# Hash-masked attention and a mixture of experts in one launch: the order of POOL's work before the first expert, and where the raw pieces of its w2 are kept

## The chip, the cores and the metric

The kernel runs on one core of one Trainium2 chip, as one program. The metric is the device time of an execution in microseconds (us); the median of three runs of the kernel before is 697.48 us (697.29 to 697.7).

Engines are named as in the profile: PE is the matmul engine (PEld its weight loads), DVE is VectorE, ACT is ScalarE, POOL is GpSimd, SP issues most of the DMAs. Each engine works through its own queue in order.

## The reference

Attention over 4 batches x 8 heads, 768 tokens, head size 64. A query sees a key only where the signs of six projections of the two agree. Its output is a matrix x of 3072 tokens x 512, and each token goes to the expert with the highest gate logit:

```python
scores = scale * np.matmul(q, k.transpose(0, 1, 3, 2))
scores = np.where(mask, scores, -1000000000.0)          # mask: equal buckets
attn = np.exp(scores - np.max(scores, axis=-1, keepdims=True))
attn = attn / (np.sum(attn, axis=-1, keepdims=True) + 1e-09)
x = np.matmul(attn, v)                                   # then 3072 x 512
...
e_idx = np.argmax(x @ w_gate, axis=1)
for e in range(E):
    h = np.maximum(x[mask] @ w1[e], 0.0)                 # 512 x 1024
    ye = h @ w2[e]                                       # 1024 x 512
    out[mask] = gate_w[mask, None] * eom[mask, e, None] * ye
```

## The kernel before

All matrix products are in float32 accuracy by way of two parts: an operand is split into a rounded high part (a copy to the type fp32r) and a low part (operand minus high part), and three products are summed.

**Attention.** The 32 heads are worked on as 16 pairs, and each pair in 12 steps, 192 steps in all. A step is one 128 x 768 block of scores: PE makes the scores (line 612), VectorE takes them out of PSUM with a row minimum (line 615), ScalarE takes the exponential and the row sums (line 623), POOL multiplies by the reciprocal of the row sums (`normal`, line 633), PE transposes the block six steps later (line 662), ScalarE, and VectorE for some, copy the transposes into the tiles `pts0` and `pts1` (lines 664 and 669), and after each six steps PE multiplies them by v (`weighted`, line 680). `normal` handles two steps at a time. In every block of six steps POOL normalises four tiles at the block's first step and two more at its fifth. Here a *tile* is such a 128 x 768 block.

**The order.** Nothing is left to a scheduler: the program is issued in the order in which it is written. `plan(step, fn)` puts a piece of work behind a step, `block(step, when, fn)` puts it at a place of the first step of a block of six (`early`, `amid`, `before`, `matmuls`, `behind`). `late` is 168. The last two blocks begin at steps 186 and 192; step 192 holds no new scores, only what is still in flight.

**The seam.** The expert with the most tokens of the first three batches is chosen at step 172 and is worked on first, with the first 256 of its tokens. During the last blocks of attention the kernel gathers these tokens (`early_gather`, step 186, two indirect DMAs issued by POOL once VectorE has made their numbers `gid`), loads the four pieces of the expert's w1 (`early_load`, 512 KB each, issued by SP into two buffers `w_raw` in turn, so piece 2 waits for the splits of piece 0 and piece 3 for those of piece 1), and splits each piece in two halves of 512 columns into high and low parts on POOL (`early_w1(cc, h)`, lines 1014 and 1015). Below, half (1,1) is the second half of piece 1.

After step 192's block the first products of the expert begin: `fill(f)` is a 128 x 256 block of x @ w1 and `low` takes its low part out of PSUM (line 369). Between them stand the last `weighted` products, the last logits (`add_pair`, lines 735 and 736), and the routing of the last batch on VectorE (`best`, line 743 is the subtraction `df`; `choose` to `ohb`; `prefix` on PE, line 797). The four pieces of w2 (two row blocks of 128 each, 512 KB) are loaded by `w2_piece` just behind `fill(0)`: two raw pieces into a spare buffer of `pts0`, two into `w_raw`. Their high and low parts are shared out by `split_weights` (lines 180 to 183): "h" puts the high part on POOL, otherwise ScalarE has it; "l" puts the low part on POOL, otherwise VectorE has it.

For every later expert, raw pieces of w1 and w2 go in turn into four buffers (two `w_raw`, `xh0`, `xlo0`); the turn is counted by the list `raws`, which grows only where `load_weights` gets no buffer handed in.

Of the kernel before, what the change touches and what calls it, by code (L numbers as in the profile page):

```python
# [21 lines left out]
P = 128  # L22
NT = S // P
HS = S // 2
DM = H * D
# [34 lines left out]
def lsh_attention_then_moe(  # L60
# [375 lines left out]
    with ExitStack() as actx:  # L436
# [24 lines left out]
        def plan(step, *fns):  # L461
            at.setdefault(step, []).extend(fns)
# [164 lines left out]
        def normal(s0):  # L627

            rs = sp.tile([P, GROUP], F32, name="rsum")
            nc.vector.tensor_reduce(rs, sums.pop(s0 // GROUP), AX.X, ALU.add)  # L630
            nc.vector.reciprocal(rs, rs)
            for k in range(GROUP):
                nc.gpsimd.tensor_scalar(live[s0 + k], live[s0 + k], rs[:, k:k + 1], 0.0, ALU.mult, ALU.add)  # L633

        def transposed(s, pr):
            g, hf, t, j = tile_of(s)
# [370 lines left out]
        def early_load(cc):  # L1007
            early.setdefault("raw", []).append(w1_load(0, cc))
            early.setdefault("w1", []).append([wpool.tile([P, F], F32R, name="w1" + n, bufs=NCC) for n in "hl"])

        def early_w1(cc, h):
            c = slice(h * F // 2, (h + 1) * F // 2)
            hi, lo, raw = (x[:, c] for x in (*early["w1"][cc], early["raw"][cc]))
            nc.gpsimd.tensor_scalar(hi, raw, 1.0, 0.0, ALU.mult, ALU.add)
            nc.gpsimd.tensor_tensor(lo, raw, f32(hi), ALU.subtract)

        plan(late + 2, compare, pick)
# [2 lines left out]
        for a in range(EARLY):  # L1020
            block(late + 24, ("early", "amid")[a], lambda a=a: early_turn(a))
        for cc in range(NCC):
            plan(late + (4, 5, 11, 15)[cc], lambda cc=cc: early_load(cc))
            for h in range(2):
                if cc >= NCC // 2 and h:
                    block(late + 24, "behind", lambda cc=cc, h=h: early_w1(cc, h))
                else:
                    plan(late + (9, 10, 13, 14, 18, 0, 20)[2 * cc + h], lambda cc=cc, h=h: early_w1(cc, h))

        with tc.manual_schedule(engines=MANUAL | {mybir.EngineType.SP}):  # L1030
            t = signs()
# [92 lines left out]
                lows.pop(0)()  # L1124

            fill(0)
            spare = tp.tile([P, NT, HS], F32, name="pts0").rearrange("p a b -> p (a b)")
            pieces = {}
            for f in (4, 6, 0, 2):
                raw = spare[:, (f - 4) * DM:(f - 2) * DM].rearrange("p (f d) -> p f d", f=2) if f >= 4 else None  # L1130
                pieces[f] = w2_piece(ep, 0, f, "h" if f >= 4 else "l", raw)
            for f in range(0, NFB, 2):
                w2s += pieces[f]
            for c in range(NT):
                weighted(2 * NP - 1, c)
                if c == 0:
# [249 lines left out]
```

## Time and profile before

| what | value |
|---|---|
| median of 3 runs | 697.48 us (697.29 to 697.7) |
| the profiled execution | 696.61 us |
| its span, first to last instruction | 694.9 us |
| DVE, ACT, POOL busy | 460.9, 440.0, 417.9 us (66, 63, 60%) |
| granted PE clock, mean | 0.998 of full speed |
| DMA, mean over the span | 126 GB/s |

Busy times are of the profiled execution. Attention takes up to about 376 us of it, the experts the rest. Times in the rows further down are us from the start of the span; a row gives the start, the length of the group in us, the engine, the line, the operation, what it writes and reads, a count, and in brackets the engine's idle time ahead of it with what ended that.

### The profile page before, as it was taken

To read this page: it belongs to the slowest core of one execution; us is meant where nothing else is said; L and a number is where in the kernel's file an instruction comes from. 1 tells how busy PE (TensorE), PEld (TensorE's weight loads), DVE (VectorE), ACT (ScalarE), POOL (GpSimd) and SP (SyncE) were. 2 spreads that over 40 slices of the span, in tenths; PEclk is the share of its full clock that TensorE was granted. 3 is DMA by queue.
4 is the path that set the end of the run, shared out by engine and by line. 5 is a ranking of instruction groups with operands and counts; after the bars stand their busy time and mean duration, and the time that the engine had idled before them with its cause. 6 is when DMAs were issued, how large, how long until landed. Compare 5 with 4: busy or idle time off the path is not lost. (4 is left out here: it accounts for less than half of the span.)

```text
span 694.9 us, 17362 instructions
## 1 busy us (share of the span) xinstructions
PE 683.1 (98%) x6591; PEld 539.3 (78%) x6591; DVE 460.9 (66%) x1012; ACT 440.0 (63%) x896; POOL 417.9 (60%) x548
## 2 busy tenths in 40 slices
PE   8999999999999999999999999999999999999996
PEld 5667676767666766666666888889999999989896
DVE  7888887888887889788876934462536354556440
ACT  5988998889888988888986224433435252434231
POOL 6767766587856678657899447163372827374201
PEclk9999999999999999999999999999999999999999
DMA  5554554364444444443444136533455444535401
GB/s 175 150 129 98 129 130 97 75 141 112 110 118 99 117 99 121 99 99 73 134 112 139 34 122 207 208 109 117 142 167 167 164 159 165 171 126 212 153 11 44
DMA packets 85283, 87.47 MB, mean 126 GB/s; under 512 B 57167, under 2 KB 67591, under 8 KB 85192
## 3 DMA queue, kind: packets, MB, share of 16 engines
q1 hardware_dynamic: 79704, 72.88, 38.5%
q0 software_dynamic: 5200, 13.31, 5.8%
q8 instruction: 54, 0.88, 0.5%
q14 instruction: 37, 0.30, 0.1%
q10 hardware_dynamic: 288, 0.10, 0.1%
HBM read 59.57 MB, written 13.11 MB: 105 GB/s over the span
## 5 line engine op out<-in xcount | busy, mean ns | idle before, releaser
L633 POOL TENSOR_SCALAR sc<-sc,rsum 128x768 f32<-128x768 f32 x192 | 171.9, 911 | 79.9 <-ACT pts L669 40.2
L615 DVE TENSOR_SCALAR_CACHE_REDUCE sc<-ps_s 128x768 f32<-128x768 f32 x192 | 176.3, 955 | 24.1 <-PE ps_s L612 22.3
L623 ACT ACTIVATE sc<-sc,mn 128x768 f32<-128x768 f32 x192 | 178.9, 951 | 3.8 <-DVE sc L615 3.7
L612 PE MATMUL ps_s<-kh,qhl 64*128 64x384 f32 x768 | 148.2, 400 | 1.4 <-DVE sc L615 0.8
L680 PE MATMUL ps_a<-pts,vt 128*64 128x384 f32 x768 | 131.2, 490 | 0.0
L669 ACT COPY pts<-ps_t 128x384 f32<-128x384 f32 x188 | 93.0, 494 | 25.3 <-PE ps_s L662 22.0
L369 DVE SCALAR_TENSOR_TENSOR hl<-ps_s,hh 128x256 fp32r<-128x256 f32 (+8 forms) x40 | 34.0, 849 | 107.6 <-ACT hh L368 107.6
L680 PEld LDWEIGHTS ps_a<-pts,vt 128*64 128x64 f32 x768 | 52.5, 137 | 66.3 <-issue 60.9
L380 POOL DMA_INDIRECT out_dram<-yo,sid x29 | 30.7, 1059 | 113.9 <-ACT yo L375 52.2
L662 PEld LDWEIGHTS ps_t<-ident,sc 64*128 64x128 f32 x1140 | 81.9, 139 | 22.1 <-POOL sc L633 13.2
L358 PE MATMUL ps_s<-xh,w1h 128*128 128x256 f32 (+7 forms) x288 | 96.8, 336 | 0.4 <-DVE hl L369 0.4
L332 POOL DMA_INDIRECT xq<-x_dram,idx x75 | 82.2, 1096 | 23.8 <-issue 21.0
L358 PE MATMUL ps_s<-xlo,w1h 128*128 128x256 f32 (+7 forms) x288 | 95.4, 331 | 0.0
L358 PE MATMUL ps_s<-xh,w1l 128*128 128x256 f32 (+7 forms) x288 | 95.3, 331 | 0.0
L662 PE MATMUL ps_t<-ident,sc 64*128 64x64 f32 x1140 | 86.9, 223 | 1.3 <-POOL sc L633 1.3
L368 ACT ACTIVATE hh<-ps_s 128x256 fp32r<-128x256 f32 (+8 forms) x40 | 29.0, 726 | 90.4 <-PE ps_s L358 90.4
L612 PEld LDWEIGHTS ps_s<-kh,qhl 64*128 64x128 f32 x768 | 76.2, 187 | 4.4 <-DVE sc L615 2.2
L612 PE MATMUL ps_s<-kl,qhl 64*128 64x384 f32 x384 | 66.6, 333 | 0.0
L612 PE MATMUL ps_s<-bb 64*128 64x384 bf16 x384 | 65.3, 327 | 0.0
L669 ACT COPY pts<-ps_m 128x384 f32<-128x384 f32 x94 | 45.1, 480 | 17.5 <-PE ps_m L662 16.1
L358 PEld LDWEIGHTS ps_s<-xh,w1h 128*128 128x128 f32 x288 | 54.2, 188 | 2.3 <-issue 0.6
L358 PEld LDWEIGHTS ps_s<-xlo,w1h 128*128 128x128 f32 x288 | 54.2, 188 | 1.4 <-DVE xlo L315 0.2
(250 smaller groups left out, 1388.4 us busy)
## 6 DMA issues: line engine op xcount, KB each, us to landing
w_raw<-in_w_dram SPq DMA_DIRECT2D x34, 512.0 KB
qk<-in_qkT_dram SPq DMA_DIRECT2D x32, 384.0 KB
qhl<-qhl SPq DMA_DIRECT2D x62, 192.0 KB
xh<-in_w_dram SPq DMA_DIRECT2D x14, 512.0 KB
xlo<-in_w_dram SPq DMA_DIRECT2D x14, 512.0 KB
vt<-in_v_dram SPq DMA_DIRECT2D x16, 384.0 KB
x_dram<-xb SPq DMA_DIRECT2D x60, 96.0 KB
xq<-x_dram,idx POOLq DMA_INDIRECT x75, 3.0
```

The lines of the kernel that those rows point to most:

```text
L332: nc.gpsimd.indirect_dma_start(out=xq[:, k * P:(k + 1) * P], out_offset=None, in_=x_dram.rearrange("n (a f) -> (n a) f", a=NB32), in_offse ...
L358: nc.tensor.matmul(ps, l, r, start=first and k == 0, stop=last and k == len(pairs) - 1)
L368: nc.scalar.activation(hh, ph, AF.Relu)
L369: return lambda: nc.vector.scalar_tensor_tensor(hl, ph, 0.0, f32(hh), ALU.max, ALU.subtract)
L380: nc.gpsimd.indirect_dma_start(out=out[:, :], out_offset=bass.IndirectOffsetOnAxis(ap=sid[0:n, r, a:a + 1], axis=0), in_=yo[0:n], in_offse ...
L612: nc.tensor.matmul(ss[:, h, 0:HS], q[rs, c:c + P], k[rs, 0:HS], start=(i == 0), stop=(i == 3))
L615: nc.vector.tensor_scalar(sc, ss[:, :, 0:HS], MASKED, None, ALU.min, ALU.min, accum_out=mn)
L623: nc.scalar.activation(pr, pr, AF.Exp, bias=mn, scale=-1.0, accum_out=sums[s // GROUP][:, k, 0:1])
L633: nc.gpsimd.tensor_scalar(live[s0 + k], live[s0 + k], rs[:, k:k + 1], 0.0, ALU.mult, ALU.add)
L662: nc.tensor.transpose(trs[h][:, c], pr[r, c * P:(c + 1) * P], ident[r, r])
L669: (nc.vector.tensor_copy if h and s and (last or s % PER == 0) else nc.scalar.copy)(pts[:, :, t * P + h * hq:t * P + (h + 1) * hq], trs[h])
L680: nc.tensor.matmul(st["av"][j * D:(j + 1) * D], st["v"][:, j, c], blocks[hb][j][:, c], start=(c == 0), stop=(c == NT - 1))
```

## The change

Four edits in the seam:

1. Half (1,1) of w1 moves from step 182 to step 186, behind the gathers and three tiles. The load of piece 3 moves from step 183 to step 186, behind that half.
2. One tile, step 184, is normalised by VectorE.
3. The high part of half (2,0) moves to ScalarE, and the half from step 186 to 187. Halves (2,1) and (3,1) move from the block of step 192 to behind the w2 pieces.
4. All four raw pieces of w2 go into spare buffers `pts0` and `pts1`. POOL makes the high parts of the first two, ScalarE those of the other two, and VectorE all four low parts. With two fewer entries in `raws`, every later piece takes the buffer two further on in the ring.

```diff
             for k in range(GROUP):
-                nc.gpsimd.tensor_scalar(live[s0 + k], live[s0 + k], rs[:, k:k + 1], 0.0, ALU.mult, ALU.add)
+                e = nc.vector if s0 + k == NSTEP - PER - GROUP else nc.gpsimd
+                e.tensor_scalar(live[s0 + k], live[s0 + k], rs[:, k:k + 1], 0.0, ALU.mult, ALU.add)
...
             hi, lo, raw = (x[:, c] for x in (*early["w1"][cc], early["raw"][cc]))
-            nc.gpsimd.tensor_scalar(hi, raw, 1.0, 0.0, ALU.mult, ALU.add)
+            if (cc, h) == (2, 0):
+                nc.scalar.copy(hi, raw)
+            else:
+                nc.gpsimd.tensor_scalar(hi, raw, 1.0, 0.0, ALU.mult, ALU.add)
             nc.gpsimd.tensor_tensor(lo, raw, f32(hi), ALU.subtract)
...
         for cc in range(NCC):
-            plan(late + (4, 5, 11, 15)[cc], lambda cc=cc: early_load(cc))
+            plan(late + (4, 5, 11, 18)[cc], lambda cc=cc: early_load(cc))
             for h in range(2):
-                if cc >= NCC // 2 and h:
-                    block(late + 24, "behind", lambda cc=cc, h=h: early_w1(cc, h))
-                else:
-                    plan(late + (9, 10, 13, 14, 18, 0, 20)[2 * cc + h], lambda cc=cc, h=h: early_w1(cc, h))
+                if cc < NCC // 2 or h == 0:
+                    plan(late + (9, 10, 13, 18, 19, 0, 20)[2 * cc + h], lambda cc=cc, h=h: early_w1(cc, h))
...
             fill(0)
-            spare = tp.tile([P, NT, HS], F32, name="pts0").rearrange("p a b -> p (a b)")
-            pieces = {}
-            for f in (4, 6, 0, 2):
-                raw = spare[:, (f - 4) * DM:(f - 2) * DM].rearrange("p (f d) -> p f d", f=2) if f >= 4 else None
-                pieces[f] = w2_piece(ep, 0, f, "h" if f >= 4 else "l", raw)
+            spare = [tp.tile([P, NT, HS], F32, name=f"pts{n}").rearrange("p a b -> p (a b)") for n in range(2)]
             for f in range(0, NFB, 2):
-                w2s += pieces[f]
+                raw = spare[f // 4][:, f % 4 * DM:(f % 4 + 2) * DM].rearrange("p (f d) -> p f d", f=2)
+                w2s += w2_piece(ep, 0, f, "h" if f < 4 else "", raw)
+            for cc in (2, 3):
+                early_w1(cc, 1)
```

The order on POOL, from half (1,0) of w1 on (`sc` are tiles, `w1h` and `w1l` the parts of a half, `xg` the gathers, `w2h` and `w2l` the parts of w2 pieces). Before:

```order
L1014 TENSOR_SCALAR w1h<-w_raw 128x512
L1015 TENSOR_TENSOR w1l<-w_raw,w1h 128x512
L1014 TENSOR_SCALAR w1h<-w_raw 128x512
L1015 TENSOR_TENSOR w1l<-w_raw,w1h 128x512
L633 TENSOR_SCALAR sc<-sc,rsum 128x768 x2
L295 DMA xg<-x_dram,gid_7521 128x512 x2
L633 TENSOR_SCALAR sc<-sc,rsum 128x768 x4
L1014 TENSOR_SCALAR w1h<-w_raw 128x512
L1015 TENSOR_TENSOR w1l<-w_raw,w1h 128x512
L1014 TENSOR_SCALAR w1h<-w_raw 128x512
L1015 TENSOR_TENSOR w1l<-w_raw,w1h 128x512
L633 TENSOR_SCALAR sc<-sc,rsum 128x768 x6
```

The same place after the change, on to the w2 pieces and the two halves behind them:

```order
L1018 TENSOR_SCALAR w1h<-w_raw 128x512
L1019 TENSOR_TENSOR w1l<-w_raw,w1h 128x512
L634 TENSOR_SCALAR sc<-sc,rsum 128x768 x2
L295 DMA xg<-x_dram,gid_7515 128x512 x2
L634 TENSOR_SCALAR sc<-sc,rsum 128x768 x3
L1018 TENSOR_SCALAR w1h<-w_raw 128x512
L1019 TENSOR_TENSOR w1l<-w_raw,w1h 128x512 x2
L1018 TENSOR_SCALAR w1h<-w_raw 128x512
L1019 TENSOR_TENSOR w1l<-w_raw,w1h 128x512
L634 TENSOR_SCALAR sc<-sc,rsum 128x768 x6
L180 TENSOR_SCALAR w2h<-pts_7893 128x1024 x2
L1018 TENSOR_SCALAR w1h<-w_raw 128x512
```

The pair of tiles and the gathers have moved up by one half, and a tile has gone from the four. Half (1,1), the low part of (2,0) and half (3,0) stand together ahead of the last six tiles. The last row begins half (2,1), which now stands behind the w2 high parts; the two low parts of w2 that followed them on POOL are gone.

On VectorE, at the last transposes of attention and the start of the routing of the last batch (`pts` copies end the attention, `w2l` are low parts of w2 pieces, `lgt` the logits, `hl` low parts of `fill`). After the change:

```order
L670 COPY pts_7776<-ps_t 128x6x64
L728 TENSOR_REDUCE lgt<-ps_t 128x48
L183 TENSOR_TENSOR w2l<-pts_7893,w2h 128x1024 x2
L183 TENSOR_TENSOR w2l<-pts_7894,w2h 128x1024 x2
L693 STREAM_TRANSPOSE xb<-ot 128x384
L737 TENSOR_TENSOR lgt<-lgt,ps_m 128x48
L684 COPY ot<-ps_a 128x384
L369 SCALAR_TENSOR_TENSOR hl<-ps_s,hh 128x256
L737 TENSOR_TENSOR lgt<-lgt,ps_m 128x48
```

Before, one row of two low parts stood there; now there are two such rows. All of them stand ahead of the copy of `ot`, which PE needs for the last logits.

On SP, from the load of piece 2 of w1 to the raw pieces of w2 (`x_dram<-xb` writes x). After the change:

```order
L173 DMA w_raw<-in_w_dram 128x1024
L700 DMA x_dram<-xb 32x24x32 x4
L173 ISA
L173 DMA w_raw<-in_w_dram 128x1024
L700 DMA x_dram<-xb 32x24x32 x4
L163 ISA
L163 DMA pts_7893<-in_w_dram 128x1024
```

The rows are those of before in the same order; the second `w_raw` row (piece 3) now waits for half (1,1) at its new place, and the four loads of w2 behind it all go to `pts`.

## Rows read from the trace of the kernel before

**Rows 1.** The page, busy time of each engine.

```profile
PE 683.1 (98%) x6591; PEld 539.3 (78%) x6591; DVE 460.9 (66%) x1012; ACT 440.0 (63%) x896; POOL 417.9 (60%) x548
```

**Rows 2.** Busy time by stretch, 391 to 690 us; columns as the first line says.

```profile
core 0: us, PE busy (x) PEld busy (x) DVE busy (x) ACT busy (x) POOL busy (x), PEclk, DMA share, GB/s
391.00:690.00 299.00, 298.68 (x1638) 278.18 (x1637) 143.70 (x190) 108.53 (x135) 132.68 (x135) 1.00 0.43 142
```

**Rows 3.** Timeline of PE, its waits in the seam.

```profile
364.15 0.27 PE L662 MATMUL ps_t<-ident,sc 64*128 64x64 f32 x1 [0.84 <-POOL sc L633]
365.03 0.27 PE L662 MATMUL ps_t<-ident,sc 64*128 64x64 f32 x1 [0.29 <-POOL sc L633]
...
389.95 0.20 PE L797 MATMUL ps_m<-ohb,tri 128*128 128x48 bf16 x1 [0.84 <-DVE ohb L762]
...
390.74 0.39 PE L358 MATMUL ps_s<-xh,w1h 128*128 128x256 f32 x1 [0.44 <-DVE hl L369]
```

**Rows 4.** Timeline of POOL, from half (1,1) on.

```profile
356.68 0.62 POOL L1014 TENSOR_SCALAR w1h<-w_raw 128x512 fp32r<-128x512 f32 x1
...
358.68 1.79 POOL L633 TENSOR_SCALAR sc<-sc,rsum 128x768 f32<-128x768 f32 x2
360.66 1.21 POOL L295 DMA_INDIRECT xg<-x_dram,gid  x1 [0.19 <-issue]
...
363.18 3.55 POOL L633 TENSOR_SCALAR sc<-sc,rsum 128x768 f32<-128x768 f32 x4
```

**Rows 5.** Timeline of DVE, the gathers' numbers, and from the w2 low parts on.

```profile
357.80 0.92 DVE L957 CAST gid<-o_gd 128x2 uint32<-128x2 f32 x1
...
380.88 3.18 DVE L183 TENSOR_TENSOR w2l<-pts,w2h 128x1024 fp32r<-128x1024 f32 x2 [2.96 <-POOL w2h L180]
...
384.57 0.54 DVE L683 COPY ot<-ps_a 128x384 f32<-128x384 f32 x1
...
386.90 1.82 DVE L743 TENSOR_TENSOR df<-lgt,mx 128x48 f32<-128x48 f32 x1
```

**Rows 6.** Timeline of POOL, half (3,0), the last six tiles, the w2 parts.

```profile
368.66 0.62 POOL L1014 TENSOR_SCALAR w1h<-w_raw 128x512 fp32r<-128x512 f32 x1
...
370.63 5.31 POOL L633 TENSOR_SCALAR sc<-sc,rsum 128x768 f32<-128x768 f32 x6
...
379.80 2.05 POOL L180 TENSOR_SCALAR w2h<-pts 128x1024 fp32r<-128x1024 f32 x2
383.19 5.46 POOL L183 TENSOR_TENSOR w2l<-w_raw,w2h 128x1024 fp32r<-128x1024 f32 x2 [1.34 <-ACT w2h L182]
```

**Rows 7.** Timeline of ACT, high parts of two w2 pieces.

```profile
382.06 1.05 ACT L182 CAST w2h<-w_raw 128x1024 fp32r<-128x1024 f32 x1 [2.63 <-DMA w_raw<-in_w_dram]
384.52 1.05 ACT L182 CAST w2h<-w_raw 128x1024 fp32r<-128x1024 f32 x1 [1.41 <-DMA w_raw<-in_w_dram]
```

**Rows 8.** Timeline of SP, loads of w1 piece 3 and of two w2 pieces.

```profile
358.72 0.36 SPq L173 DMA_DIRECT2D w_raw<-in_w_dram  x1
...
377.92 0.33 SPq L173 DMA_DIRECT2D w_raw<-in_w_dram  x1
...
379.86 0.33 SPq L173 DMA_DIRECT2D w_raw<-in_w_dram  x1
```

**Rows 9.** Busy time by stretch, from the issue of piece 3's load on.

```profile
358.72:361.75 3.03, 3.03 (x40) 1.54 (x38) 1.22 (x6) 1.67 (x6) 2.84 (x3) 1.00 0.50 173
```

**Rows 10.** Timeline of PE, the last tile's transposes and the last logits.

```profile
376.35 0.59 PE L662 MATMUL ps_s<-ident,sc 64*128 64x64 f32 x12
...
385.43 0.75 PE L735 MATMUL ps_m<-wgt,ot 128*128 128x32 f32 x6
```

**Rows 11.** Timeline of DVE at the start of the kernel.

```profile
8.37 1.25 DVE L546 SCALAR_TENSOR_TENSOR qhl<-qk,qhl 128x384 fp32r<-128x384 f32 x1
```

**Rows 12.** Timeline of POOL at the same time.

```profile
8.02 1.19 POOL L548 TENSOR_TENSOR kl<-qk,kh 128x384 fp32r<-128x384 f32 x1
9.18 0.81 POOL L555 TENSOR_SCALAR qhl<-qk 128x384 fp32r<-128x384 f32 x1
9.96 0.51 POOL L556 TENSOR_SCALAR kh<-qk 128x384 fp32r<-128x384 f32 x1
```

## The prediction

> **What bounds the kernel now.** I read the page's totals first, then the releasers of the matmul engine's idle time, then the timelines of the engines around those waits. PE is busy for 683.1 us of a 694.9 us span [rows 1]: only removing PE idle time can help. From 391 us to the end PE shows 298.68 us busy in 299 [rows 2], so what the change does to the later experts can gain nothing, and what it moves must pay in the seam between attention and the first expert. There PE has four large idle entries [rows 3]: 0.84 and 0.29 us at 364 to 365, waiting for softmax tiles that POOL normalises, and 0.84 and 0.44 us at 390, waiting for VectorE's routing chain: 2.41 us together. The others in the seam are 0.2 us or less. That is the whole stake, plus what each wait hides at an engine's start.
>
> The POOL timeline [rows 4] says why PE waits at 364: the second half of w1 piece 1 (its high part from 356.68, then its low part) stands ahead of a pair of tiles at 358.68, then come two gathers from 360.66, and only at 363.18 the tiles that PE wants. The VectorE timeline [rows 5] says why PE waits at 390: the subtraction `df` takes 1.82 us on 48 columns, from 386.90 to 388.72, and it ends as POOL's two w2 low parts end, 383.19 + 5.46 = 388.65 [rows 6].
>
> **The change, step by step.**
> *POOL before the load.* Half (1,1) leaves, so the tile pair starts at 356.68 and ends 1.79 later, at 358.47 [rows 4]. The gathers need `gid`, which VectorE ended at 357.80 + 0.92 = 358.72 [rows 5]; that cast sat beside POOL's instruction too, and I keep 358.72. With 0.2 us to start, the gathers run from 358.9; they took 363.18 - 360.66 = 2.52 us, so 361.4. Three tiles instead of four, 3.55 / 4 = 0.89 each: 364.1. PE wants the first of them at 364.15 - 0.84 = 363.3, and it is there at 362.3, so the waits of 0.84 and 0.29 go. The fourth tile lies on VectorE, which at that time waits for PE: nothing on PE's path. ScalarE's new cast (half of the 1.05 us of a whole piece [rows 7], about 0.55) stands ahead of four PSUM copies of the tiles that are now early; ScalarE had to wait for those tiles before, so this too costs PE nothing against before.
>
> *The wait that the change adds.* Piece 3 of w1 is now loaded after half (1,1), whose raw buffer it takes over. High and low part of a half take 370.63 - 368.66 = 1.97 us [rows 6]: (1,1) ends at 364.1 + 1.97 = 366.1, and SP can issue the load only then; before, it was issued at 358.72 [rows 8], some ten us ahead of POOL's reader at 368.66. Now the reader, the high part of (3,0), comes right behind it, and **behind that stand the last six softmax tiles**. How long does the load take? No row shows a lone load with its waiting reader, so by bounds: the one issued at 358.72 had traffic until 361.75 (173 GB/s for 3.03 us, which is 524 KB) [rows 9], so 3.0 us at least; for the ones issued at 377.92 and 379.86 ScalarE waited until 382.06 and 384.52 [rows 7, 8], 4.14 and 4.66 us. I take 4.14, the reader that waited least: 370.2. The low part of (2,0) fits into that wait. Then (3,0), 1.97: 372.2, and six tiles, 5.31 [rows 6]: **377.5, where before they ended at 370.63 + 5.31 = 375.9**. PE's transposes of the last tile start at 377.5, not 376.35 [rows 10]; with their 0.59 us what follows starts at 378.1. Before, it was 0.17 us later than that after them, behind ScalarE's copy, at 377.1. PE has lost its gain and is 1.0 us behind. It is due at the last logits (line 735) at 385.43 + 1.0 = 386.4.
>
> *The low parts of w2.* POOL goes on with two high parts, 2.05 us [rows 6]: 379.5. VectorE now has four low parts. Two took 3.18 us from 380.88, but the first stood until POOL's casts ended (379.80 + 2.05 = 381.85), so they take (384.06 - 381.85) / 2 = 1.1 us each [rows 5, 6]. Against them POOL now runs halves (2,1) and (3,1). Do they overlap? At the start of the kernel VectorE's operation at 8.37 takes 1.25 us beside POOL's at 8.02, and POOL's next, dispatched at 9.18, takes 0.81 where the same shape takes 0.51 at 9.96 [rows 11, 12]: the two engines took turns, and the waiting one came in although the other had its next one queued. I take turns here too: 4 x 1.1 + 0.62 + 1.35 + 0.62 = 7.0 us (a half's 1.97 less its high part's 0.62 are the 1.35), so 386.5. Ahead of PE's logits come then a transpose and the copy of `ot`; from the end of the low parts at 384.06 to the end of that copy, 384.57 + 0.54, it was 1.05 us [rows 5]: 387.55, and PE starts at 387.6, not 386.4: a **new wait of 1.2 us**, 2.2 us behind before.
>
> *What is paid back.* From 385.43 to 390.74 PE needed 5.31 us, of which 0.84 + 0.44 idle [rows 3, 10]: 4.03 of work. The chain on VectorE is shorter: POOL's long low parts are gone, and of the 1.82 us of `df` all but 0.07 lie before their end, so I take 1.6 off, and the 389.95 - 385.43 = 4.52 us to the end of the chain become 2.9. Ready at 390.5, wanted some 3 us after 387.6, at 390.6 or later: hardly a wait. PE stands at 387.6 + 4.03 = 391.6 where it was at 390.74: +0.9.
>
> *The buffers.* The raw pieces of later experts change places in a ring of four; the first two of expert 1 go to `w_raw` and are loaded earlier. PE is not idle there [rows 2], so nothing.
>
> **Sum:** -1.1 (waits at 364) + 2.1 (late last tiles) + 1.2 (low parts) - 1.3 (waits at 390) = +0.9 us. The profiled execution took 696.61 us, so 697.5; the median of the runs is 0.87 above it, so **698.4**. About 0.2% (1.4 us) is what a measurement of this kernel tells from no change, so this reads as the same.
>
> The Trainium skill ("SBUF — State Buffer", section "SBUF: two separate sides") says that a VectorE instruction with two SBUF inputs and a POOL instruction that reads SBUF contend for a port pair, an exclusive lock that whichever starts first holds for its whole instruction. The trace agrees: 1.82 us for `df`. By that rule the sum stands as it is; if the engines overlapped, it would be rival A's.
>
> **Rivals.**
> *A, VectorE keeps the upper hand for its four low parts.* For it: its second low part followed the first although POOL had asked at 383.19 [rows 5, 6]. Against it: rows 11 and 12. They end at 379.5 + 4.4 = 383.9, the copy of `ot` is in time, the logits run at 386.4, and PE stands at 386.4 + 4.03 = 390.4: -0.3, **697.2**.
> *B, faster: A and a quick load.* With the load at its lower bound, 3.0 us, all POOL times come 1.1 earlier: -0.3 - 1.1 = -1.4, and 0.2 more if the gathers start at once: **695.9**. It decides below a load of some 3.1 us. Against it: both reads of rows 7.
> *C, slower: the gathers and the load both meet company.* VectorE's new tile falls on the first gather; its price lies between nothing and the 0.89 us that POOL took for such a tile. The x writes that follow on SP's queue can stretch the load to 4.66. A tenth on POOL is a tenth at the end: +0.9 with 0.5 for each is +1.9, with all of both +2.3: **699.4 to 699.8**. It decides once half a us is added. For it: the first gather took 1.21 us [rows 4].
> The Trainium skill (same page and section, the trap "DVE blocks DMA") says that POOL is kept from writing a gather's descriptors while VectorE runs a two-port operation; no run here shows it for this tile.
> *D, the gathers do not move.* If something other than POOL's queue held them at 360.66, all of POOL is 1.8 later: +2.7, **700.2**, and the change would not do what it says.
>
> **Chances.** Forecast 0.40, A 0.18, B 0.10, C 0.27, D 0.05. Faster by over 0.2%: B and a little of A, 0.12. Slower by over 0.2%: C, D and the upper end of the forecast (a load of 4.66 us), 0.40. Within: 0.48. The range leaves out the quicker part of B, D and the end of C: 696.1 to 700.0. The forecast's own, with the load between 3.7 and 4.66 us, is 698.0 to 698.9.
>
> **What would show it.** Right: no PE wait at 364; POOL idle for about 3 us in front of the high part of (3,0), released by the load; PE idle between the transposes of the last six tiles; PE waiting for the copy of `ot` ahead of the last logits; `df` at 0.2 us and no wait for the end of its chain. Wrong: if POOL waits under 2 us for the load, or the four low parts run in 4.5 us, the time is under 697.5; if the first of the three tiles starts after 362, it is over 699.

## The result, and the profile after

The change makes the kernel **slower**: 702.58 us (median of 6, 700.49 to 704.0) against 697.98 us for the kernel before on the same chip, a ratio of 1.0062 (95% interval 1.0048 to 1.0077). The forecast was 698.4 us, its range ended at 700.0. The profiled execution is the quickest of the six, 700.49 us with a span of 698.8 us: 3.9 us more than before's.

PE's idle time, as in [rows 1, 2]: first the page's totals, then the stretch from 391 us on (columns as in [rows 2]).

```profile
PE 684.2 (98%) x6591; PEld 539.6 (77%) x6591; DVE 462.9 (66%) x1015; ACT 439.9 (63%) x897; POOL 414.7 (59%) x544
```

```profile
391.00:690.00 299.00, 296.94 (x1623) 276.34 (x1623) 142.88 (x190) 108.09 (x135) 132.79 (x135) 1.00 0.43 142
```

Before, PE idled 0.32 us in that stretch; now 2.06 us, in a part of the kernel in which no line of code was changed. The timeline of PE shows its waits (the answer to [rows 3]; three more like the first ones are left out):

```profile
373.14 0.59 PE L663 MATMUL ps_t<-ident,sc 64*128 64x64 f32 x12 [0.39 <-POOL sc L634]
374.03 0.59 PE L663 MATMUL ps_s<-ident,sc 64*128 64x64 f32 x12 [0.30 <-POOL sc L634]
...
377.55 0.59 PE L663 MATMUL ps_s<-ident,sc 64*128 64x64 f32 x12 [0.29 <-POOL sc L634]
...
387.00 0.86 PE L736 MATMUL ps_m<-wgt,ot 128*128 128x32 f32 x6 [0.45 <-DVE ot L684]
...
409.71 0.72 PE L306 MATMUL ps_t<-ident,xg 128*128 128x128 f32 x4 [2.06 <-DMA xg<-x_dram,gid]
```

The waits at 364 and 390 are gone, the last six tiles come late one after another, the copy of `ot` is late: the seam, as forecast. The last line is new and was not forecast: PE waits for a gather, the second half of the first expert's later tokens (`xg`).

POOL in the seam, which answers to [rows 4, 6]:

```profile
356.74 1.78 POOL L634 TENSOR_SCALAR sc<-sc,rsum 128x768 f32<-128x768 f32 x2
358.85 1.30 POOL L295 DMA_INDIRECT xg<-x_dram,gid  x1 [0.33 <-DVE rsum L631]
...
361.46 2.68 POOL L634 TENSOR_SCALAR sc<-sc,rsum 128x768 f32<-128x768 f32 x3
...
370.21 0.62 POOL L1018 TENSOR_SCALAR w1h<-w_raw 128x512 fp32r<-128x512 f32 x1 [2.88 <-DMA w_raw<-in_w_dram]
...
372.17 5.32 POOL L634 TENSOR_SCALAR sc<-sc,rsum 128x768 f32<-128x768 f32 x6
...
379.48 1.59 POOL L1018 TENSOR_SCALAR w1h<-w_raw 128x512 fp32r<-128x512 f32 x1
381.15 2.11 POOL L1019 TENSOR_TENSOR w1l<-w_raw,w1h 128x512 fp32r<-128x512 f32 x1
```

and VectorE ([rows 5]):

```profile
378.80 7.10 DVE L183 TENSOR_TENSOR w2l<-pts,w2h 128x1024 fp32r<-128x1024 f32 x4
...
386.40 0.54 DVE L684 COPY ot<-ps_a 128x384 f32<-128x384 f32 x1
...
388.57 0.21 DVE L744 TENSOR_TENSOR df<-lgt,mx 128x48 f32<-128x48 f32 x1
```

SP's loads ([rows 8]): piece 3 of w1, then what matters, the first two loads of the second expert:

```profile
366.12 0.36 SPq L173 DMA_DIRECT2D w_raw<-in_w_dram  x1
...
401.66 1.01 SPq L173 DMA_DIRECT2D w_raw<-in_w_dram  x2
```

Before, SP issued no load between 392 and 422.95 us (there `xh` was the first). The DMA issues between 399 and 412 us, first of before, then of the change (tile, queue, count, KB each for loads, median us to landing):

```profile
xg<-x_dram,gid POOLq DMA_INDIRECT x5, 3.4
out_dram<-yo,sid POOLq DMA_INDIRECT x2, 2.9
```

```profile
w_raw<-in_w_dram SPq DMA_DIRECT2D x2, 512.0 KB
xg<-x_dram,gid POOLq DMA_INDIRECT x4, 6.8
out_dram<-yo,sid POOLq DMA_INDIRECT x1, 6.2
```

Gathers and the scatter take twice as long beside 1 MB of loads. The Trainium skill ("DMA: Bandwidth & Descriptors", section "Issuing engines are not separate DMA queues") says that DMAs of different issuing engines run on the same 16 DMA engines and interleave; these rows agree.

### The profile page after: what moved, and what is told of

It is laid out like the page before. It is cut to its first block, busy times and chain, and to the rows that moved or that the text cites. A ratio compares the mean times of both kernels' runs of the same rounds, so it can differ in the third digit from the quotient of the medians.

```text
span 698.8 us, 17358 instructions
## 1 busy us (share of the span) xinstructions
PE 684.2 (98%) x6591; PEld 539.6 (77%) x6591; DVE 462.9 (66%) x1015; ACT 439.9 (63%) x897; POOL 414.7 (59%) x544
```

## The experiments

Theory T: the loads at 401.66 are the loss. Rival S: the seam's own new waits are. C and D are about the spread of the executions, O and P about how the loads do harm, T2 about the program's end. All times are medians, beside before on the same chip; chips differ by up to 2.7 us for before. The ratio is estimated from the executions and need not be the quotient of the two medians.

| run | us | before | ratio (95%) |
|---|---|---|---|
| e1_ring_back | 699.62 | 698.79 | 1.0019 (1.0006 to 1.0033) |
| e2_ring_only | 698.98 | 698.79 | 1.0006 (0.9992 to 1.0021) |
| e3_loads_held | 699.58 | 698.79 | 1.0025 (1.0009 to 1.0041) |
| e4_tiles_first | 699.75 | 698.79 | 1.0025 (1.0013 to 1.0037) |
| a2_change_again | 703.15 | 698.78 | 1.0068 (1.0042 to 1.0094) |
| e6_ring_and_gap | 699.05 | 698.78 | 0.9998 (0.9983 to 1.0013) |
| e7_gather_early | 701.44 | 698.78 | 1.0039 (1.0024 to 1.0053) |
| e5_two_lows_late | 698.44 | 698.78 | 0.9996 (0.9981 to 1.0010) |
| b2_before_again | 697.36 | 698.24 | 0.9993 (0.9981 to 1.0005) |
| e8_lows_placed | 697.21 | 698.24 | 0.9993 (0.9978 to 1.0007) |
| e9_pe_kept_busy | 701.12 | 698.24 | 1.0048 (1.0028 to 1.0069) |
| e10_placed_ring | 702.28 | 698.24 | 1.0065 (1.0039 to 1.0090) |
| e13_before_no_rounds | 700.27 | 700.65 | 0.9991 (0.9978 to 1.0005) |
| e12_change_no_rounds | 701.59 | 700.65 | 1.0021 (1.0006 to 1.0035) |
| e14_seam_alone | 700.75 | 700.65 | 1.0004 (0.9989 to 1.0019) |
| e11_pick_early | 699.02 | 700.65 | 0.9974 (0.9962 to 0.9986) |
| a3_change_third | 703.22 | 698.50 | 1.0059 (1.0041 to 1.0076) |
| e1b_ring_back_again | 699.01 | 698.50 | 1.0016 (1.0003 to 1.0028) |

To see where in the span each profile gains or loses, I lined the traces up: the start of the 181st score tile on VectorE (344.0 us in before) is taken as zero, and the table gives how far PE's results are behind before's (us; less is earlier) at the end of ScalarE's relu of the eighth fill, of the first product behind the fills, at the dispatch of the last scatter, and the time from there to the span's end (before: 4.33).

| profile | eighth fill | next product | last scatter | rest |
|---|---|---|---|---|
| the change | -0.05 | +2.26 | +2.26 | 5.89 |
| a2_change_again | +1.43 | +2.99 | +4.25 | 5.85 |
| a3_change_third | +0.95 | +5.00 | +5.02 | 6.04 |
| e1_ring_back | +0.82 | +0.83 | +0.87 | 5.72 |
| e1b_ring_back_again | +2.20 | +2.23 | +2.26 | 5.94 |
| e3_loads_held | +0.97 | +0.97 | +0.97 | 5.90 |
| e2_ring_only | +0.01 | +0.05 | +0.96 | 5.69 |
| e6_ring_and_gap | +0.03 | +0.54 | +1.94 | 4.32 |
| e7_gather_early | +0.43 | +0.46 | +2.08 | 5.98 |
| e4_tiles_first | +0.98 | +1.00 | +1.02 | 5.79 |
| e8_lows_placed | -2.32 | -2.33 | -1.14 | 5.70 |
| e10_placed_ring | -2.35 | -2.38 | +4.05 | 6.11 |
| e11_pick_early | -2.38 | -2.35 | -0.51 | 5.86 |

### Is it the loads or the seam?

**e1_ring_back**, and again beside the change itself as **e1b_ring_back_again**; the edit is one line behind the loop over w2's pieces:

```diff
                 w2s += w2_piece(ep, 0, f, "h" if f < 4 else "", raw)
+            raws += [0, 1]
```

> The change as it is, but the ring of raw buffers goes on where it did before: expert 1's first two loads go to xh0 and xlo0 again and so are issued at some 423 us, not 401.66. Theory T (the two loads at 401.66 run beside the gathers of the first expert's last tokens, which land after up to 7.4 us instead of 3.5, and PE waits 2.1 us for them at 409.7): that wait is gone, no load is issued on SP between 392 and 420 us, and the time is that of before, 697.0 to 698.5 us. Rival S (the ring costs nothing, as predicted; the seam's own new waits are the loss): as the change, 701 to 703 us.

> The change with the ring set back, beside the change on the same chip. Theory T (the early loads are the largest part of the loss, by the gathers and scatters that they slow): 2 to 4 us under the change, 0.5 to 2.0 us over before, of which 1.4 us are the program's end by the profiles and the rest the seam's. If the ring is worth what the two runs without the unused block say (0.8 us): 3 us or more over before, within 1.5 us of the change.

The change's own third run stood beside the second of these:

> The change once more, on the same chip as the run with the ring set back, to have the ring's price from one chip. Whatever the chip, 4 to 5 us over before if the program's end (1.5 us in the profiles), the early loads and the seam add up as in the first two comparisons (1.0062 and 1.0068).

With the list two entries longer, the second expert's loads start in `xh0` again, are issued at 424.29, and the gathers land after 3.6 us (e1: SP's first load behind 396 us, then the DMA issues between 399 and 412 us):

```profile
424.29 0.39 SPq L173 DMA_DIRECT2D xh<-in_w_dram  x1
```

```profile
xg<-x_dram,gid POOLq DMA_INDIRECT x4, 3.6
out_dram<-yo,sid POOLq DMA_INDIRECT x2, 3.0
```

On one chip: change 703.22, ring set back 699.01, before 698.50. **By the medians the ring is worth 4.2 us of the 4.7 us that the change loses there**; rival S falls. The size is less sure than the cause: the executions spread over 2.9 us (the change, 6 of them) and 4.1 us (e1b, 12), and their means differ by 2.9 us. e1 lay 1.1 us over theory T's upper end, e1b 0.2 us outside one of its ranges and at the lower edge of the other: a loss of 0.5 to 0.8 us stays without the loads.

**e3_loads_held** keeps the ring and holds the loads until the tokens have landed:

```diff
+        for i in range(2):
+            held = wpool.tile([P, F], F32, name="w_raw", bufs=2)
+            nc.sync.dma_start(held[0:1, 0:4], xg[1][0][0:1, 0:4])
```

> The change, with its ring, but the two loads are held until the first expert's gathered tokens have landed: 16 bytes of them are copied into each w_raw buffer first, so that the loads have to wait for that. Theory T: the gathers land after 3.5 us as before, the loads are issued at about 406 to 408 us, PE does not wait at 409, and the time is 697.0 to 699.0 us. Rival S: as the change, 701 to 703 us. If the gathers' lateness comes from something other than the loads, it stays in this run and goes in none of those that keep the change's seam.

The loads go out at 408.84, the gathers land after 3.7 us, PE does not wait for them: 699.58, like e1 and not like the change, though half a us over the range. So it is the moment of the loads, not the buffer they go to.

**e2_ring_only** is before with the ring turned (`del raws[-2:]` behind the same loop).

> The kernel before with one thing of the change alone: the ring of raw buffers is turned by two, so that expert 1's first two loads go to w_raw. Theory T: the loads are issued at about 400 us, PE waits about 2 us for the gathered tokens at about 409, and the time is 2 to 5 us over before: 699.5 to 702.5 us. Rival S: as before, 697.5 to 698.5 us.

A miss of theory T as it stood: 698.98, 0.2 us over before and not told apart from it. The loads were issued at 401.94 and the gathers landed after 5.9 us, yet PE did not wait for them. Its profile loses 0.9 us later on, since POOL's scatter waited for the slowed one ahead of it and `pick`, POOL's copy of a selection matrix that stands behind it, came late (timeline of PE):

```profile
416.07 1.08 PE L324 MATMUL ps_t<-tacc,pick 128*128 128x32 f32 x8 [0.62 <-POOL pick L320]
```

### Why the same loads hurt the change and not before

The two gathers and VectorE's rows around them, in before and in the change (timelines of DVE and POOL):

```profile
399.39 0.17 DVE L957 CAST gid<-o_gd 128x2 uint32<-128x2 f32 x1
...
399.80 0.41 DVE L982 TENSOR_REDUCE tacc<-o_tt 128x32 f32<-128x256 f32 x1
...
399.83 1.02 POOL L295 DMA_INDIRECT xg<-x_dram,gid  x1 [3.68 <-DVE gid L957]
401.16 0.95 POOL L295 DMA_INDIRECT xg<-x_dram,gid  x1 [0.30 <-issue]
```

```profile
399.26 0.42 DVE L983 TENSOR_REDUCE tacc<-o_tt 128x32 f32<-128x256 f32 x1
399.59 0.16 DVE L958 CAST gid<-o_gd 128x2 uint32<-128x2 f32 x1
...
399.99 0.60 DVE L981 TENSOR_TENSOR o_tt<-tacc_e,perm 128x256 f32<-128x256 f32 x1
...
400.03 1.41 POOL L295 DMA_INDIRECT xg<-x_dram,gid  x1 [3.81 <-DVE gid L958]
401.75 0.95 POOL L295 DMA_INDIRECT xg<-x_dram,gid  x1 [0.30 <-issue]
```

In the change the reduction stands ahead of the cast `gid`. No line of that code differs: behind the seam VectorE's order is not simply the written one, as my description of the kernel had it (in before, too, a first `o_tt` runs at 398.68, ahead of the cast that is written before it). The next two-input operation, `o_tt`, is then already running when the first gather starts, and the gather takes 1.41 us instead of 1.02, in every profile with that order. So the second gather is dispatched 0.09 us behind the loads, where in e2 it is 0.73 ahead of them (401.21 and 401.94). Of these 0.82 us the longer gather makes 0.39; it also starts 0.15 later, and the loads go out 0.28 earlier. The Trainium skill ("SBUF — State Buffer", section "SBUF: two separate sides", the trap "DVE blocks DMA") says that POOL cannot write a gather's descriptors while VectorE runs an operation in a two-port mode, such as a copy. `o_tt` is a product of two SBUF inputs, which the trap does not name; the row shows a delay of that kind for it too, 0.39 us.

**e7_gather_early** puts the cast back ahead in the change:

```diff
+            nc.vector.tensor_copy(tacc[0:1, 0, 0, 0:1], gid0[0:1, 0:1])
             for i in (0, 2, 1):
```

> The change with its ring and its seam, but VectorE casts the gather's numbers ahead of the reduction of the expert table, as before (one element of the table is first written from those numbers). In the change the cast stands behind that reduction, and a VectorE operation with two inputs runs over the first gather, which takes 1.41 instead of 1.02 us. Theory O: the first gather is dispatched at 399.8 and takes 1.0 us, the second is dispatched at about 401.2, ahead of the loads at 401.7, it lands after about 6 us, PE waits less than 0.5 us at 409, and the time is 1.5 to 2.5 us under the change's: 699 to 700.5 us. Rival P (the loads alone, whatever the order): PE still waits about 2 us, and the time is the change's.

The first gather takes 1.02 us, the second is dispatched 0.94 us ahead of the loads, PE does not wait for it, and the median is 1.7 us under a2's on that chip, though at 701.44 it is 0.9 us over the expected range, and the two intervals in the table overlap. The profile shows that the order makes the wait for the tokens; what it is worth in the median is less sure, and it is not all of the price: PE waits 0.5 us for `pick` here, as in e2.

**e6_ring_and_gap** tries the opposite in e2, a POOL copy between the two gathers:

```diff
-        xg = [gather(gid0[:, a:a + 1]) for a in range(EARLY)]
+        xg = [gather(gid0[:, 0:1])]
+        gap = mp.tile([P, 512], F32, name="gap")
+        nc.gpsimd.tensor_copy(gap, ident[:, None, :].broadcast_to([P, 4, P]))
+        xg.append(gather(gid0[:, 1:2]))
```

> The kernel before with the ring turned, and a copy of 0.65 us on POOL between the first expert's two late gathers. In the run with the ring alone the second gather was dispatched at 401.21, ahead of the loads (401.94), and landed after 5.9 us, and PE did not wait; in the change it is dispatched at 401.75, behind the loads (401.66), lands after 7.4, and PE waits 2.1 us. Theory O (what costs is that the second gather falls behind the loads): here it is dispatched at about 402.0, lands at 408.5 to 409.5, PE waits 1 to 2.5 us at 409, and the time is 1.5 to 3 us over the run with the ring alone: 700.5 to 702 us. Rival P (the gap by itself is harmless and the ring's price in the change comes from elsewhere): PE does not wait at 409 and the time stays at 698.5 to 699.5.

Inconclusive: the second gather went out at 402.51, still 0.15 us ahead of the loads, so the case was not made. PE waited 0.2 us.

**e10_placed_ring** turns the ring in a kernel (e8, below) whose gathers are a us earlier.

> The kernel with the low parts placed, but with the ring turned as in the change, so that expert 1's two loads go to w_raw right behind the choice of the experts. There VectorE casts the gather's numbers over a us ahead of the expert order, so both gathers are dispatched well ahead of the loads. Theory O (the ring costs what it does where the second gather is dispatched behind the loads): no wait for the tokens, within 0.5 us of the kernel with the ring as before. Rival P (loads this early always cost): 2 to 3.5 us over it.

Rival P, and beyond its range: 702.28 against e8's 697.21 on the same chip, 5.1 us. The gathers were early enough, the scatters were not (timelines of POOL and PE):

```profile
412.43 0.99 POOL L385 DMA_INDIRECT out_dram<-yo,sid  x1 [5.46 <-DMA out_dram<-yo,sid]
...
415.98 0.64 POOL L325 COPY pick<-ident 128x512 f32<-128x512 f32 x1
...
416.67 1.70 PE L329 MATMUL ps_t<-tacc,pick 128*128 128x32 f32 x7 [3.47 <-POOL pick L325]
```

Not all of this is the wait of 3.47 us. Behind it the granted clock is at its lower level for about 6.8 us (in stretches of 2 us from 414 to 424 its mean is 0.94, 0.50, 0.50, 0.50 and 0.85), which costs an estimated half of that; all six executions have a mean clock of 0.994 to 0.996.

The loads slow the gathers and scatters that lie beside them, and which one PE then waits for depends on what it needs next: the tokens in the change, the scatter's queue here.

### What the executions of the change differ in

The six executions of the first comparison fall into two groups: 700.49 and 701.04 us at a mean granted clock of 0.998, and 702.4 to 704.0 us at 0.993 to 0.995.

> The change itself once more, beside the kernel before on the same chip, to see what differs between its executions (spans of 698.8 to 702.3 us, mean granted clock 0.998 to 0.993). Theory C (after a stretch in which PE idles much, at 372 to 378 or at 409 us, the granted clock goes to half for some 3 us, in some executions and not in others, as the rows of the two runs with a mean clock of 0.996 show at 379 to 382 and at 388 to 391): if the profiled execution has a mean clock under 0.998, its rows show one such stretch of half clock per 0.002 to 0.003, behind idle PE; each costs some 1.5 us. Theory D (the spread is in the loads and gathers alone): the wait at 409 differs between the executions, the clock does not. Median 701 to 703 us.

703.15 us, just over the range, but the profile of that run was at 0.998, with other losses: PE waited 1.8 us for `ot` and 1.3 for the tokens. In the later runs time and clock do not go together so neatly (702.48 us at 0.999 in a2, 701.25 us at 0.994 in a3). The profile of **a3_change_third** (span 701.9, clock 0.993) is at the lower clock. Its stretches, columns as in [rows 2], and its wait for the tokens:

```profile
376.00:378.00 2.00, 1.19 (x26) 0.92 (x26) 0.79 (x3) 1.51 (x3) 2.00 (x4) 1.00 1.00 363
378.00:380.00 2.00, 2.00 (x19) 1.88 (x20) 0.80 (x3) 1.01 (x2) 2.00 (x3) 0.53 0.97 377
380.00:382.00 2.00, 2.00 (x12) 1.86 (x13) 2.00 (x2) 0.06 (x1) 1.92 (x2) 0.61 0.09 37
...
410.00:412.00 2.00, 0.73 (x5) 0.76 (x6) 0.00 (x0) 0.00 (x0) 0.00 (x0) 1.00 0.53 211
412.00:414.00 2.00, 2.00 (x6) 1.54 (x6) 0.69 (x1) 0.58 (x1) 0.00 (x0) 0.57 0.06 25
414.00:416.00 2.00, 2.00 (x12) 1.99 (x11) 0.00 (x0) 0.69 (x1) 0.78 (x1) 0.58 0.00 0
```

```profile
411.27 0.72 PE L306 MATMUL ps_t<-ident,xg 128*128 128x128 f32 x4 [2.38 <-DMA xg<-x_dram,gid]
```

Behind both stretches in which PE idles much (the late tiles, the late tokens) the granted clock falls from 2.4 to 1.2 GHz: 0.53 and 0.61, then 0.57 and 0.58 are about 3.4 us each at the lower level. Behind the tokens PE loses 4.05 us here (+0.95 to +5.00); 2.4 are the wait, the rest the clock. In the change's first profile waits of nearly the same length (2.06 us for the tokens) stand without the fall.

**e9_pe_kept_busy** gives PE work whose result is overwritten:

```diff
+            if last:
+                nc.tensor.transpose(trs[0][:, 0], ident[0:hq], ident[0:hq, 0:hq])
...
+        for i in range(idles):
+            nc.tensor.transpose(px[:, i % NCC], ident, ident)
...
+                    turn(xg[f // 2 - 1], x0, (f // 2 - 1) * CH, 8 if f == 4 else 0)
```

> The change, with PE given something to do where it waits: one transposition more (of the identity, its result is overwritten) ahead of each of the last six tiles, and eight ahead of the tokens that come late at 409. Nothing else is moved and the late tiles and late tokens stay. Theory C (in some executions the granted clock falls to half for 3.4 us after the idle stretches, which is most of what the slower executions of the change have over its fastest): the median comes to 700.0 to 701.5 us, the spread shrinks, and the profile shows full clock. Theory D (the clock's falls don't matter, the loads and gathers vary): 702.5 to 704 us, as the change, or more for PE's added work.

701.12 us, 1.5 to 2.1 us under the change's three runs, with a clock of 0.997 and no fall in its profile: inside theory C's range. But the interval of its ratio overlaps those of the change's three runs, and the spread did not shrink: five executions took 699.5 to 701.1 us and four 702.7 to 704.4, three of these at 0.992 and one at 0.994. That the added work makes the fall rarer is not shown, nor that the clock alone makes an execution long.

### The end of the program

In the change the span ends 5.89 us after the dispatch of the last scatter, in before 4.33. The DMA queues from just before that dispatch to the end, before and then the change:

```profile
q14 instruction: 4, 0.03, 2.3%
```

```profile
q14 instruction: 5, 0.04, 2.3%
```

> The kernel before itself, for a second profile of it: the first one ended 4.33 us after the last scatter's dispatch, all but one of the later profiles of other kernels 5.7 to 6.0 us after theirs. If that is an accident of the execution, this profile shows either value, and the ratio to before is 1.000 within 0.2%; if the kernels differ there, it shows 4.3 again.

4.24 us: near the first value, so it goes with the kernel. All profiles with the changed seam and this code at the end have one more 8 KB instruction load there, and 5.7 to 6.2 us. Only e2, with before's seam and four loads, has 5.69, so the load alone does not explain the longer end; what does is open. Three runs left out the unused extra rounds that stand last in the code:

```diff
-    with tc.If(nr > 0):
...
```

> The kernel before without the block behind the last expert (the loop of extra rounds for experts with more tokens than planned, which these inputs don't enter), so that the program ends behind the last scatter. It leaves those rounds out. It is the base for the two runs of the change without the block. Theory T2 (the change's span ends 5.9 us after its last scatter's dispatch and before's 4.3, because two instruction loads of 8 KB follow it in the one and one in the other; it is where the program's end falls in its code, no work): some 0.5 to 2.5 us under before, as the jump over the block is gone, and the last scatter is followed by about the same time as in the other two runs.

> The change without that block, ring turned as in the change; the extra rounds are left out. Theory T2: the time from the last scatter's dispatch to the end is the same as in the run of before without the block within 0.3 us, and the change is 2.3 to 3.3 us over that run (the wait for the tokens, and the half clock in some executions), 1.3 us less than the 4.4 to 4.6 it is over before. Otherwise (the end's 1.5 us belong to the change): 4.0 to 4.8 us over that run.

> The change without that block and with the ring set back: the seam's edits alone, without the early loads and without what comes at the program's end; the extra rounds are left out. The prediction's sum for the seam is +0.9 us: 0.4 to 1.4 us over the run of before without the block. If the seam in truth costs nothing, as the profiles at the fifth fill show it (0.0 us in two, 0.4 to 1.5 in three): 0.0 to 0.5.

The rest is now 4.62 us in the first and 5.02 in the other two: the end differs by 0.4 us, not 1.56. The change is 1.3 us over before here, the seam alone 0.5 us, each without the block. That leaves 0.8 us for the ring, less than expected, and with executions that spread over more than 4 us neither 0.8 nor 0.5 is told apart from nothing. In e12's profile PE waited 1.0 us for the tokens and lost 1.3 us there, not 2.3; why the wait is shorter is open. All three profiles, that of before without the block among them, lose another 1.4 to 1.5 us at about 430 us, in part ahead of rows released by "issue" (time in which PE waited for nothing that the profile shows): that loss belongs to no edit.

### A version that beats both

**e4_tiles_first** is e1 with half (3,0) behind the last six tiles on POOL:

```diff
+                if (cc, h) == (3, 0):
+                    block(late + 24, "before", lambda cc=cc, h=h: early_w1(cc, h))
-                if cc < NCC // 2 or h == 0:
+                elif cc < NCC // 2 or h == 0:
```

> The change with the ring set back (as in the run that only does that), and half (3,0) of w1 moved on POOL behind the last six tiles, so that POOL need not wait for the load of piece 3 ahead of them. By the steps of the prediction: the six tiles run from about 367.4 and end at 372.7, the transposes of the last six tiles have no waits (1.8 us in the change), the copy of ot is in time, and the time is 1.5 to 2.5 us under before: 695.3 to 696.5 us. Theory S: the ring back does nothing, so 699 to 701 us. If the tiles' lateness was covered by something else anyway: 697.5 to 698.5 us.

A miss: the tiles' waits went as expected, and what they had hidden came up, the copy of `ot` behind four low parts:

```profile
386.73 0.85 PE L736 MATMUL ps_m<-wgt,ot 128*128 128x32 f32 x6 [2.34 <-DVE ot L684]
```

and behind it the clock fell for 3.4 us. **e5_two_lows_late** moves two of the low parts (those marked "d", kept in a list `late_lows`) behind the routing's gates and columns, **e8_lows_placed** to where VectorE was idle; the diff is of e8:

```diff
+                w2s += w2_piece(ep, 0, f, "h" if f < 4 else "d", raw)
...
             fill(1)
             low()
+            late_lows.pop(0)()
...
             gid0 = lead_slots(EARLY)
             low()
+            late_lows.pop(0)()
```

> The run with the tiles first (ring set back, half (3,0) behind the last six tiles), and two of VectorE's four low parts of w2 moved behind the routing's chain: one behind the gates, one behind the columns. There PE waited 2.3 us for the copy of ot, which stood behind the four low parts, and the granted clock then fell to half for 3 us. By the steps of the prediction: the copy of ot is in time (before 385.0), PE waits under 0.5 us ahead of the last logits, the chain is in time, and PE is 2 to 2.5 us ahead of before at 392; the gathers at 400 come no later than 402, which PE doesn't want before 407. Time 695 to 697 us, with the mean clock at 0.998. If it stays within 698.5 to 699.5, PE's idle time there was not what the seam costs.

> The tiles-first kernel with VectorE's last two low parts of w2 placed where VectorE was idle: one between the copy of ot and the last logits (1.31 us of idleness in the run with two lows late), one behind the first expert's gather numbers. In that run PE waited 0.53 us at 391 and 0.72 us at 395 for VectorE's work behind the two late low parts, and was 3.1 us ahead of before at the fifth fill, 1.2 us at the first product of the experts. Expected: both waits gone, PE some 3 us ahead of before at the eighth fill, no half clock; 695.0 to 697.0 us, faster than before by 0.25 to 0.5%. Rival: what is gained is lost again behind the seam, where the loads and gathers of the next expert come no earlier: 698 to 699 us.

e5 missed by 1.4 us: its low parts delayed the chain by 0.5 and 0.7 us. In e8 PE is 2.3 us ahead of before at the eighth fill, and loses 1.2 us of it to `pick`; its median, 697.21, is 0.2 us above the range, and not told apart from before. **e11_pick_early** makes `pick` ahead of the gathers:

```diff
+        pick = new_pick()
         xg = [gather(gid0[:, a:a + 1]) for a in range(EARLY)]
```

> The kernel with the low parts placed, ring as before, and POOL's copy of the selection matrix made ahead of the gathers, where POOL is idle, not behind the scatter that waits for the one ahead of it: PE, 2.25 us ahead of before at that point, waited 0.9 us for it and lost 1.2. Expected: that wait gone, PE 2.0 to 2.3 us ahead of before at the last scatter, and the span under before's by that less the 1.4 us of the program's end: 696.0 to 697.2 us against before's 697.4 to 698.8, faster by 0.1 to 0.3%. If something else is late next, it stays at 697.2 to 698.2.

**699.02 us against 700.65 on that chip, 0.9974 (0.9962 to 0.9986): faster than before by 0.26%**, as expected by the ratio. The expected times were missed by 1.8 us, but before takes some 2 us longer on that chip too. PE is still 2.35 us ahead behind the fills, and loses 1.8 us at about 430 us (1.1 of it ahead of rows released by "issue"), as the others on that chip do.

## Why the prediction was wrong

By its own steps:

- *POOL before the load.* Right: tiles from 356.74, gathers from 358.85, three tiles to 364.12, no wait at 364. VectorE's tile cost nothing that PE sees.
- *The wait that the change adds.* Right: load issued at 366.12 (forecast 366.1), its reader at 370.21 (370.2), the six tiles to 377.49 (377.5), PE idle between their transposes. At the relu of the second fill PE is 0.91 us behind before (1.0).
- *The low parts of w2.* Right in kind, too dear: the engines took turns, but VectorE began at 378.80, before POOL's second high part had ended, and its 7.10 us ended at 385.90, not 386.5. The copy of `ot` ended at 386.94, not 387.55, so PE waited 0.45 us, not 1.2, and at the fourth fill it is 1.63 us behind, not 2.2. In a2 the wait was 1.8 us: this term varies.
- *What is paid back.* Right in kind, too little: `df` 0.21 us, no wait at the chain's end, and 1.6 us paid back by the fifth fill, not 1.3.
- The seam's sum, +0.9 us, was -0.05 to +1.43 in the change's three profiles, and +0.5 us, not told apart from nothing, by e14 over e13. The size stood, in part by luck. Where PE waited about 0.5 us for `ot` and the clock held, the seam cost -0.05 to +0.43 us (the change, e7, e12). It cost +0.97 and +1.43 where that wait was 0.9 and 1.8 us (e3, a2). In e14, e1, a3 and e1b the clock fell behind the late tiles, for about 3.4 us and in e1b 6.8; PE, late by that, did not wait for `ot`, and the seam cost +0.36, +0.82, +0.95 and +2.20. The sum has no term for the clock.
- ***The buffers* failed**: "PE is not idle there [rows 2], so nothing." The row shows that nothing can be gained there. It does not show how late PE's inputs may come. Moved from 422.95 to 401.66, two loads fell on the gathers and the scatter, which need 3.4 and 2.9 us alone and 6.8 and 6.2 beside them, and PE had asked for the second half of the tokens at 407.65. The runs give this term, instead of nothing, 4.2 us in the medians on one chip. In the profiles, from the eighth fill to the next product, it is 1.6 and 2.3 us in two runs of the change and 4.05 in the third, where the clock fell behind the wait; e12 over e14, without the block at the end, gives 0.8 us within the noise, the ring in the kernel before (e2) 0.2, and in e8's kernel (e10), by way of the scatter, 5.1. So the step's sign and mechanism are shown; its size goes with what waits beside the loads.
- Not in the sum: the granted clock, which falls behind idle stretches in some executions, and the program's end. Ring set back, what is left over before is 0.5 to 0.8 us in the median; the single profiles would give the end alone 1.4. How much of the end stays in a median is open.

None of the rivals had this mechanism; C was on the slower side for the seam's reasons, and those did not cost it.

## What to carry to other kernels

A busy engine's row says what cannot be won, not what can be lost: for each transfer that a change issues earlier, list the gathers, scatters and loads in the stretch where it now lies, with issue, landing and the moment they are wanted. A counter that picks buffers in turn is part of the schedule, so that leaving out two entries moves every later load. And compare the whole order on each engine, also where no line was changed: here one swapped pair on VectorE put a gather behind the loads.

## What the runs showed of the hardware that I had not expected

Two 512 KB loads doubled the landing time of a 256 KB gather (3.4 to 6.8 us) and of a scatter (2.9 to 6.2). A gather that starts while VectorE is in the 0.60 us `o_tt` takes 1.41 us, one that starts just ahead of it 1.02. The granted clock fell to half for about 3.4 us behind a stretch in which PE was 1.2 to 1.4 us busy of every 2, and behind a single wait of 2.4 us (a3), and for about 6.8 us behind a wait of 3.5 us (e10); in another execution of the change, with 1.3 to 1.4 us busy of every 2 and a wait of 2.06 us, it did not fall.
